# Folding a query weight with 32x32 matmul tiles and DMA turns, in a fused linear-attention and expert kernel

## The chip, the cores and the metric

The kernel runs on one core of one Trainium2 chip. The metric is the device time of one execution in microseconds (us). The kernel before was run three times: 270.49, 270.82 and 271.87 us, median 270.82 us.

## The reference, cut to what matters

```python
# x: [1, 2048, 1024], 32 heads of width 32
g = sigmoid((x * gate_w).sum(-1, keepdims=True))
q, k, v = split_heads(x @ wqkv)
pq, pk = q @ w_phi[h], k @ w_phi[h]                 # per head, 32 x 32
phi = lambda p: concat([softmax(p), softmax(-p)])   # 64 features a head
kv, z = phi(pk).T @ v, phi(pk).sum(0)
a = (phi(pq) @ kv) / (phi(pq) @ z + 1e-6) @ wo
# expert path: the one row of x with the largest router score
idx = argmax(x @ w_r); xs = x[idx]
y = (silu(xs @ w_gate) * (xs @ w_up)) @ w_down * sigmoid(r[idx])
b = x with y added to row idx
out = g * a + (1 - g) * b
```

Since `pq = x @ wq @ w_phi`, the kernel first multiplies the weights: the folded weight of a head is its 32 columns of `wq` times its 32x32 `w_phi`. The same is done for `wk`.

## The kernel before

The rows of x are 16 tiles of 128, and the depth 1024 is 8 blocks `kb` of 128. `xT` holds x transposed.

**V stage.** `v_first` computes V for tiles 0 and 1, and `k_v(t, c)` for the others, in three column groups c of 256, 384 and 386 columns (the last two columns of the 386 are the router score and the gate score, kept in `rg`). A tile is 24 matmuls. Between them lie the folds. `wT_load` brings one block of `wk` or `wq` transposed (a DMA transpose) into a quarter of one of the two `shv` buffers, six blocks at a time. `fold(which, wf, kb)` multiplies it: 8 matmuls of 128x128 whose moving operand is `BDm`, a block-diagonal matrix with four heads' `w_phi`, and two VectorE casts of 512 columns out of PSUM (tag `pB`) into `wkf` or `wqf`. `FOLDS[t]` says how many folds tile t has; all 16 lie in tiles 8 to 15, the key's first. At tile 15 `route()` finds the row with the largest router score: a TensorE transpose, VectorE max and index per tile, a small DMA (`mrow`) that brings the 16 candidates into one partition, VectorE again, then SyncE reads the index and loads that row (`rows`).

**K stage.** Steps i = 0 to 31 call `feats(i, wkf, False)`: 8 matmuls of 512 columns into a PSUM buffer (`pk`, pool `psA`, two buffers), two exponentials on ScalarE, sums and reciprocals on VectorE, the product phi on GpSimd or VectorE. From step 5 on `k_kv` accumulates phi times V into `kvps`, three PSUM banks that two memsets at the end of `v_first` prepared. At i = 7 `xs_turn` turns the loaded expert row on TensorE, and ScalarE spreads it into `xs32`; at i = 8, 14 and 21 `ffn_gu` multiplies it with the gate and up weights (32 or 48 matmuls of 512 columns with 32 weight columns each, four column positions of the array side by side). Their weights lie in buffers of 1 MB: `shv` (letter D), `ring` (A, three buffers) and a buffer for the later stores (W and V).

**Q stage.** Steps 32 to 63 do `feats` with `wqf` (`pq`), a DMA transpose of phi (`q_turn`), the numerator (`q_num`) and the output projection (`q_wo`), in an order that a table of times sets.

Each engine works through its own list in order; the lists are made ahead of the run. All DMAs that SyncE (SP) issues go into one hardware queue, q1.

Of the kernel before, what the change touches and what calls it, by code (L numbers as in the profile page):

```python
# [37 lines left out]
TX = 4  # L38
FOLDS = [0] * 8 + [1, 2, 2, 2, 2, 2, 2, 3]
TDV = 0  # L40


def general_path(tc, A_wqkv, A_w_phi, A_wo, x2, out2, gate, omg, y2, idx_pool, xT, wqf, ident, BDm):
# [46 lines left out]
    def features(w):  # L90
        for hf in range(2):
            for kb in range(KB):
                nc.tensor.matmul(pp[:].rearrange("p h f -> p (h f)"), lhsT=xTt[:, kb, :],
                                 rhs=w[:, kb, hf * 512:(hf + 1) * 512], start=(kb == 0), stop=(kb == KB - 1))
            nc.vector.tensor_reduce(out=mm[:, 0, :], in_=pp[:], axis=AX.X, op=ALU.max)
            nc.vector.tensor_reduce(out=mm[:, 1, :], in_=pp[:], axis=AX.X, op=ALU.min)
            for s in range(2):
                nc.vector.tensor_tensor(out=sh[:, s], in0=pp[:], in1=_bc(mm[:, s, :], [P, HH, DH]), op=ALU.subtract)
                nc.scalar.activation(out=sh[:, s], in_=sh[:, s], func=ACTF.Exp, scale=(1.0 if s == 0 else -1.0))
            nc.vector.tensor_reduce(out=sr[:], in_=sh[:], axis=AX.X, op=ALU.add)  # L100
            nc.vector.reciprocal(out=sr[:], in_=sr[:])
            for s in range(2):
                nc.vector.tensor_tensor(out=phi[:, hf * HH:(hf + 1) * HH, s, :], in0=sh[:, s],
                                        in1=_bc(sr[:, s, :], [P, HH, DH]), op=ALU.mult)

    with tc.For_i(0, S, P) as r0:
# [6 lines left out]
        features(wkf)  # L113
# [8 lines left out]
    with tc.For_i(0, NT, 1) as t:  # L122
# [3 lines left out]
        nc.vector.tensor_copy(out=gt[:, 1:2], in_=omg[:, bass.ds(t, 1)])  # L126
        features(wqf)
        for g in range(2):
# [36 lines left out]
def kernel(  # L165
# [130 lines left out]
    def wT_load(which, kb):  # L296
        n = (which * KB + kb) % 6
        wT[which, kb] = shv[n // 4][:, n % 4, :].rearrange("p (k f) -> p k f", f=P)
# [19 lines left out]
    def route():  # L318
# [152 lines left out]
    def ffn_gu(r, bufs):  # L471
        ws = [gu_load(r, k, b) for k, b in enumerate(bufs)]
        acc = psB.tile([P, 512], F32, name="facc", tag="pB")
# [79 lines left out]
    def v_first():  # L553
# [13 lines left out]
        for t in (1, 0):  # L567
            for c in range(3):
# [4 lines left out]
                v_out(t, c, acc[t, c])  # L573
        nc.vector.memset(kvps[:], 0.0)
        nc.vector.memset(kvps[:, 0:16 * KSTR].rearrange("p (r c) -> p r c", c=KSTR)[:, :, DH:66:DH + 1], 5e-7)

    kst = {}

    def feats(u, wf, is_q):
# [3 lines left out]
        for kb in range(KB):  # L583
            nc.tensor.matmul(pkf, lhsT=xT[:, kb, t * P:(t + 1) * P], rhs=wf[:, kb, hf * 512:(hf + 1) * 512],  # L584
                             start=(kb == 0), stop=(kb == KB - 1))
# [126 lines left out]
    def wload(n):  # L712
        wn["want"] += n
        while wq and wn["done"] < min(wn["want"], wn["folded"] + 6):
            wT_load(*wq.pop(0))
            wn["done"] += 1
# [16 lines left out]
    for t in range(TX, NT):  # L733
# [3 lines left out]
        for n, c in enumerate((2, 0, 1) if t == NT - 1 else (0, 1, 2)):  # L737
            k_v(t, c)
            if c == 2 and t == NT - 1:
                route()  # L740
            if n >= 3 - FOLDS[t]:
                w, kb = fq.pop(0)
                fold(w, wkf if w == 0 else wqf, kb)
                wn["folded"] += 1
                wload(1 if t + TX >= NT else 0)
    LAG = 5
# [142 lines left out]
```

## Time and profile before

| | |
|---|---|
| median of three runs | 270.82 us (270.49 to 271.87) |
| the profiled execution | 271.42 us |
| its span, first to last instruction | 269.7 us |
| TensorE (PE) busy | 262.7 us, 97% |
| VectorE (DVE) / ScalarE (ACT) / GpSimd (POOL) busy | 195.3 / 119.4 / 128.1 us |
| granted TensorE clock, mean | 0.996 of full speed |

The profile is of one execution, whose own time lies 0.6 us above the median of the runs. A matmul's recorded duration runs to the end of its pipeline, so that neighbours overlap; what a matmul costs TensorE is read from the distance between the starts of rows.

### The profile page before, as it was taken

Reading aid. Unit: us, or ns where it says so; the run is one execution under the profiler, and the core shown is the slowest. Engines: PE = TensorE matmul, PEld = TensorE weight load, DVE = VectorE, ACT = ScalarE, POOL = GpSimd, SP = SyncE. Lnnn points to the kernel's source line nnn. Section 1 sums busy time; section 2 is a strip of 40 time slices with the busy share of each in tenths; the row PEclk is TensorE's granted clock in tenths of the full one; section 3 lists DMA queues with packets and bytes.
Section 4 is the critical chain, followed back from the end, with each engine's and each line's share of the span. In section 5 each row is a group of like instructions: output and inputs, shape, how many; then the busy total and the mean of one; then the engine's idle time right before and its main releaser. Section 6 shows DMA issues by size and latency. Waiting matters only on the chain.

```text
span 269.7 us, 5422 instructions
## 1 busy us (share of the span) xinstructions
PE 262.7 (97%) x2023; PEld 143.6 (53%) x2023; DVE 195.3 (72%) x330; ACT 119.4 (44%) x243; POOL 128.1 (48%) x113
## 2 busy tenths in 40 slices
PE   8999999999999999999999999999999999999992
PEld 4666667777544555545554444455444454454441
DVE  3020015566789896999998999889889798888772
ACT  3154333333354554545546465545355544544110
POOL 6000000000096979739779997654555535554010
PEclk9999999999999999999999999999999999999998
DMA  6999999997950699669936899899997999899642
GB/s 237 240 149 187 182 190 322 157 191 195 416 205 0 202 414 394 243 202 381 355 85 228 166 176 209 180 209 198 224 207 156 181 212 168 204 138 232 138 120 62
DMA packets 102521, 56.35 MB, mean 209 GB/s; under 512 B 85132, under 2 KB 90332, under 8 KB 102492
## 3 DMA queue, kind: packets, MB, share of 16 engines
q1 hardware_dynamic: 99692, 51.29, 78.8%
q10 hardware_dynamic: 2768, 4.67, 6.4%
q8 instruction: 17, 0.28, 0.5%
q14 instruction: 12, 0.10, 0.1%
q0 software_dynamic: 32, 0.00, 0.0%
HBM read 31.27 MB, written 4.20 MB: 132 GB/s over the span
## 4 chain that ended last, share of the span: by engine, by line
PE 91%; DVE 5%; DMA 1%; ACT 1%; issue 1%; POOL 0%
PE po L693 20%; PE pk L584 20%; PE pv L542 18%; PE pq L584 17%; PE num L654 3%; PE kvps L620 3%; PE pW L307 3%; DVE ssum L592 3%; PE facc L478 2%; PE pv L564 1%; PE kvps L564 1%; DMA shv<-in_A_x_dram 1%; DVE rq L599 1%; DVE KV L629 1%; PE small_ps L496 1%
## 5 line engine op out<-in xcount | busy, mean ns | idle before, releaser
L592 DVE TENSOR_REDUCE ssum<-e 128x32 f32<-128x1024 bf16 x64 | 76.9, 1203 | 6.4 <-ACT e L588 6.2
L605 POOL TENSOR_TENSOR phi<-e,rq 128x1024 bf16<-128x1024 bf16 x32 | 61.0, 1913 | 40.4 <-DVE rq L599 32.9
L584 PEld LDWEIGHTS <-xT 128*128 128x128 bf16 x512 | 47.3, 97 | 52.6 <-issue 1.3
L584 PE MATMUL pq<-wqf,xT 128*128 128x512 bf16 x256 | 60.3, 379 | 0.0
L693 PE MATMUL po<-wo_sb,oT 128*128 128x512 bf16 (+2 forms) x264 | 60.0, 372 | 0.0
L584 PE MATMUL pk<-wkf,xT 128*128 128x512 bf16 x256 | 59.9, 379 | 0.0
L542 PE MATMUL pv<-wv_sb,xT 128*128 128x256 bf16 (+2 forms) x336 | 52.0, 307 | 0.0
L605 POOL TENSOR_TENSOR phi<-e,rs 128x1024 bf16<-128x1024 bf16 x25 | 47.8, 1912 | 2.3 <-DVE rs L599 1.4
L542 PEld LDWEIGHTS <-xT 128*128 128x128 bf16 x336 | 31.7, 97 | 14.1
L549 ACT CAST v_all<-pv 128x384 bf16<-128x384 f32 (+1 forms) x45 | 20.1, 448 | 40.8 <-PE pv L542 35.1
L587 ACT ACTIVATE e<-pq 128x512 bf16<-128x512 f32 x32 | 19.0, 594 | 42.7 <-PE pq L584 40.7
L693 PEld LDWEIGHTS <-oT 128*128 128x128 bf16 x264 | 23.8, 98 | 23.1
L587 ACT ACTIVATE e<-pk 128x512 bf16<-128x512 f32 x32 | 19.1, 597 | 29.2 <-PE pk L584 21.4
L309 DVE CAST wkf<-pW 128x512 bf16<-128x512 f32 x16 | 10.3, 686 | 28.1 <-PE pW L307 28.1
L420 POOL COPY wch<-shv 1x1 bf16<-1x1 bf16 x3 | 0.4, 178 | 57.4 <-DMA shv<-in_A_wqkv_dram 57.4
L697 DVE SCALAR_TENSOR_TENSOR oo<-po,gate,xg 128x512 bf16<-128x512 f32 (+2 forms) x33 | 24.0, 727 | 4.1 <-PE po L693 4.0
L602 POOL TENSOR_TENSOR ksum<-ksum,ssum 128x32 f32<-128x32 f32 x32 | 14.0, 438 | 22.0 <-DVE ssum L592 20.4
L659 DVE TENSOR_TENSOR o_sb<-num,rden 128x512 bf16<-128x512 f32 x32 | 21.7, 677 | 0.8
L588 ACT ACTIVATE e<-pk 128x512 bf16<-128x512 f32 x32 | 18.9, 591 | 0.0
L588 ACT ACTIVATE e<-pq 128x512 bf16<-128x512 f32 x32 | 18.9, 590 | 0.0
L678 ACT ACTIVATE xg<-xin,omg 128x1024 f32<-128x1024 bf16 x16 | 18.3, 1148 | 0.5
L654 PEld LDWEIGHTS <-phT 128*128 128x128 bf16 x256 | 12.3, 98 | 8.6 <-issue 1.1
(132 smaller groups left out, 201.3 us busy)
## 6 DMA issues: line engine op xcount, KB each, us to landing
wch<-in_B_w_down_dram SPq DMA_DIRECT2D x7, 1024.0 KB
wch<-in_B_w_up_dram SPq DMA_DIRECT2D x6, 1024.0 KB
wch<-in_B_w_gate_dram SPq DMA_DIRECT2D x4, 1024.0 KB
xin<-in_A_x_dram ACTq DMA_DIRECT2D x16, 256.0 KB
out_dram<-oo SPq DMA_DIRECT2D x30, 128.0 KB
wch<-in_B_w_gate_dram SPq DMA_DIRECT2D x4, 768.0 KB
wv_sb<-in_A_wqkv_dram SPq DMA_DIRECT2D x8, 256.0 KB
wo_sb<-in_A_wo_dram SPq DMA_DIRECT2D x1, 2048.0 KB
```

Source lines behind the costliest of these rows:

```text
L542: nc.tensor.matmul(pv[:, 0:hi - lo], lhsT=xT[:, kb, t * P:(t + 1) * P], rhs=wv_sb[:, kb, lo:hi], start=(kb == 0), stop=(kb == KB - 1))
L549: nc.scalar.copy(out=v_all[:, t, h0:h1, 0:DH], in_=pv[:, 0:(h1 - h0) * DH].rearrange("p (h d) -> p h d", d=DH))
L584: nc.tensor.matmul(pkf, lhsT=xT[:, kb, t * P:(t + 1) * P], rhs=wf[:, kb, hf * 512:(hf + 1) * 512], start=(kb == 0), stop=(kb == KB - 1))
L587: nc.scalar.activation(out=e[:, :, 0, :], in_=pk[:], func=ACTF.Exp)
L588: nc.scalar.activation(out=e[:, :, 1, :], in_=pk[:], func=ACTF.Exp, scale=-1.0)
L592: nc.vector.tensor_reduce(out=ssum[:], in_=e2, axis=AX.X, op=ALU.add)
L605: eng.tensor_tensor(out=phi[:].rearrange("p h s f -> p (h s) f"), in0=e2, in1=_bc(rs, [P, HH * 2, DH]), op=ALU.mult)
L654: nc.tensor.matmul(num[:, pl * 66:pl * 66 + 66], lhsT=phT[:, pl, :], rhs=KV[hf][:, pl, :], start=True, stop=True)
L659: nc.vector.tensor_tensor(out=st["o"][:, hf * HH:(hf + 1) * HH, :].rearrange("p (r h) d -> p r h d", h=2), in0=nv[:, :, :, 0:DH], in1=rden ...
L678: nc.scalar.activation(out=xg, in_=st["xin"][:], func=ACTF.Copy, scale=omg[:, t:t + 1])
L693: nc.tensor.matmul(po[:, 0:w], lhsT=st["oT"][:, kb, :], rhs=moe["wo"][:, kb, sl], start=(kb == 0), stop=(kb == KB - 1))
L697: nc.vector.scalar_tensor_tensor(out=o_out[:, 0:w], in0=po[:, 0:w], scalar=gate[:, t:t + 1], in1=st["xg"][:, sl], op0=ALU.mult, op1=ALU.add)
```

## The change

The fold of `wk` keeps its form, but lies in tiles 5 to 12, one to a tile, with eight `shv` quarters in place of six. The fold of `wq` is done the other way round by `qfold`: the weights are the 32x32 blocks `w_phi` and the moving operand is the loaded `wq` block, 512 columns (four kb of 128), so that the result is the folded weight transposed. Sixteen such matmuls, one for each of the 16 positions of 32 rows by 32 columns, make a pack; they write `kvps` (three banks) and one `pB` buffer. Four packs lie in tiles 13, 14 and 15 (`PACKS`). Two VectorE and two ScalarE copies take each pack to `wfT` (two `ring` buffers), and eight DMA transposes (`qfold_turn`, steps 1 to 8) turn it into `wqf`. Its column order is now by row position r first, so the moving operand of `pq` is read through `q_heads` in pieces of 32 columns.

The preparation of `kvps` moves to ScalarE (`kv_zero`, written at step 2). The second half of `route` becomes `route_row`, written at step 0 and held behind the first reciprocal of the K stage. The first expert loads (round 0) are written at step 0, and the buffers of all four rounds are dealt out anew.

```diff
-FOLDS = [0] * 8 + [1, 2, 2, 2, 2, 2, 2, 3]
+FOLDS = [0] * 5 + [1] * 8 + [0] * 3
+PACKS = {(13, 2): (0, 0), (14, 1): (1, 0), (15, 0): (0, 1), (15, 2): (1, 1)}
...
+def q_heads(wqf, kb, hf):
+    return wqf[:, kb, hf * 512:(hf + 1) * 512].rearrange("p (r c f) -> p c r f", r=4, f=DH)
...
-        n = (which * KB + kb) % 6
+        n = kb
...
+    def qfold(a, half):
+        if (a, half) == (0, 0):
+            moe["wfT"] = [ring.tile([P, 4, D], BF, name="wfT", tag="wch") for _ in range(2)]
+        pB = psB.tile([P, 512], F32, name="pW", tag="pB")
+        banks = [kvps[:, 0:512], kvps[:, 512:1024], kvps[:, 1024:1536], pB[:]]
+        for r in range(4):
+            for c in range(4):
+                j = 4 * a + c
+                nc.tensor.matmul(banks[r][32 * c:32 * c + 32, :].rearrange("p (k d) -> p k d", d=P),
+                                 lhsT=BDm[32 * r:32 * r + 32, j, 32 * r:32 * r + 32],
+                                 rhs=shv[half][32 * r:32 * r + 32, :, j * P:(j + 1) * P],
+                                 start=True, stop=True, tile_position=(32 * r, 32 * c), skip_group_check=True)
+        for r in range(4):
+            (nc.vector.tensor_copy, nc.scalar.copy)[r % 2](out=moe["wfT"][a][:, r, half * 512:(half + 1) * 512], in_=banks[r])
+
+    def qfold_turn(ar):
+        nc.sync.dma_start_transpose(out=wqf[:, :, ar * P:(ar + 1) * P], in_=moe["wfT"][ar // 4][:, ar % 4, :])
+
+    def kv_zero():
+        one = ones[:, 0:1]
+        nc.scalar.activation(out=kvps[:], in_=one.to_broadcast([P, 3 * 512]), func=ACTF.Copy, scale=0.0)
...
+    def route_row():
+        mrow = moe["mrow"]
         mxv = const.tile([1, 1], F32, name="mxv")
+        nc.vector.tensor_copy(out=mxv[:], in_=moe["rs"][0:1, 0:1])
...
-        nc.vector.memset(kvps[:], 0.0)
-        nc.vector.memset(kvps[:, 0:16 * KSTR].rearrange("p (r c) -> p r c", c=KSTR)[:, :, DH:66:DH + 1], 5e-7)
...
-            if c == 2 and t == NT - 1:
+            if n == 1 and t == NT - 1:
                 route()
...
-            ffn_gu(r, ("AAAD", "DWVA", "AADD")[r])
+            ffn_gu(r, ("WVDD", "AAAW", "VDDA")[r])
             if r == 2:
-                ffn_gu(3, "WV")
+                ffn_gu(3, "AA")
...
+        if i == 0:
+            moe["gu0"] = [gu_load(0, k, b) for k, b in enumerate("WVDD")]
         if i == 2:
+            kv_zero()
             gates()
+        if i == 0:
+            route_row()
+        if 1 <= i <= 8:
+            qfold_turn(i - 1)
```

Two places show how the lists of the engines change. ScalarE, from the gate's exponential at the end of the V stage into the K stage, before (the numbers behind the names keep the buffers apart):

```order
L313 ACTIVATE eg_1030<-rg_114 128x16
L549 CAST v_all_111<-pv_929 128x8x32
L549 CAST v_all_111<-pv_951 128x12x32
L587 ACTIVATE e_982<-pk_973 128x16x32
L588 ACTIVATE e_982<-pk_973 128x16x32
L587 ACTIVATE e_1001<-pk_992 128x16x32
L588 ACTIVATE e_1001<-pk_992 128x16x32
```

The same place of ScalarE's list in the changed kernel:

```order
L329 CAST wfT_779<-pW_865 128x512
L329 CAST wfT_779<-kvps_140 128x512
L583 CAST v_all_111<-pv_886 128x8x32
L583 CAST v_all_111<-pv_910 128x12x32
L329 CAST wfT_780<-pW_920 128x512
L329 CAST wfT_780<-kvps_140 128x512
L621 ACTIVATE e_950<-pk_941 128x16x32
L622 ACTIVATE e_950<-pk_941 128x16x32
L336 ACTIVATE kvps_140<-const-bfloat16-1.0 128x1536
L621 ACTIVATE e_1000<-pk_991 128x16x32
L622 ACTIVATE e_1000<-pk_991 128x16x32
L337 ACTIVATE kvps_140<-const-bfloat16-1.0 128x16x2
```

The copies of the last two packs stand ahead of the exponentials of step 0, and the long write of `kvps` between those of step 0 and step 1.

SyncE, from the last weight loads of the folds to the load of the expert row, before (`wch` is an expert weight buffer, `mrow` and `rows` the router's two DMAs):

```order
L299 DMA_TRANSPOSE shv<-in_A_wqkv_dram 128x8x128 x10
L454 DMA wch<-in_B_w_gate_dram 128x2x2048 x4
L333 DMA mrow<-mi 1x16x2
L454 DMA wch<-in_B_w_gate_dram 128x2x1536
L454 DMA wch<-in_B_w_up_dram 128x2x512
L344 TENSOR_LOAD ixi
L344 ISA x2
L345 ISA
L345 DMA rows<-in_A_x_dram 8x128
```

The same place of SyncE's list in the changed kernel:

```order
L304 DMA_TRANSPOSE shv<-in_A_wqkv_dram 128x8x128 x8
L488 DMA wch<-in_B_w_gate_dram 128x2x2048 x3
L488 DMA wch<-in_B_w_gate_dram 128x2x1536
L332 DMA_TRANSPOSE wqf<-wfT 128x8x128
L362 DMA mrow<-mi 1x16x2
L488 DMA wch<-in_B_w_gate_dram 128x2x2048
L332 DMA_TRANSPOSE wqf<-wfT 128x8x128 x4
L378 TENSOR_LOAD ixi
L378 ISA x2
L379 ISA
L379 DMA rows<-in_A_x_dram 8x128
L332 DMA_TRANSPOSE wqf<-wfT 128x8x128 x3
```

Five of the eight turns and a 1 MB expert load now stand between the last loads of the V stage and the load of the expert row.

## Rows read from the trace of the kernel before

**Rows 1.** The page's first part: busy us, share of the span, instructions.
```profile
PE 262.7 (97%) x2023; PEld 143.6 (53%) x2023; DVE 195.3 (72%) x330; ACT 119.4 (44%) x243; POOL 128.1 (48%) x113
```

**Rows 2.** The page's chain that ended last, shares by line.
```profile
PE po L693 20%; PE pk L584 20%; PE pv L542 18%; PE pq L584 17%; PE num L654 3%; PE kvps L620 3%; PE pW L307 3%; DVE ssum L592 3%; PE facc L478 2%; PE pv L564 1%; PE kvps L564 1%; DMA shv<-in_A_x_dram 1%; DVE rq L599 1%; DVE KV L629 1%; PE small_ps L496 1%
```

**Rows 3.** TensorE in order of time, end of the V stage: start, us, instruction.
```profile
66.06 0.61 PE L307 MATMUL pW<-BDm,shv 128*128 128x128 bf16 x8
66.51 0.82 PE L542 MATMUL pv<-wv_sb,xT 128*128 128x256 bf16 x6
67.32 0.23 PE L321 MATMUL small_ps<-ident,r_tm 128*128 128x128 bf16 x1
...
69.80 8.80 PE L584 MATMUL pk<-wkf,xT 128*128 128x512 bf16 x40
78.43 0.42 PE L620 MATMUL kvps<-v_all,phi 128*128 128x66 bf16 x8
```

**Rows 4.** TensorE in order of time around the first expert round.
```profile
84.37 0.17 PE L350 MATMUL small_ps<-ident,rows 128*128 128x8 bf16 x1
...
86.02 1.91 PE L478 MATMUL facc<-wch,xs 128*32 128x512 bf16 x32
87.87 0.82 PE L584 MATMUL pk<-wkf,xT 128*128 128x512 bf16 x3
```

**Rows 5.** TensorE in order of time, the two score columns of a first tile.
```profile
13.64 0.34 PE L571 MATMUL pv<-wv_sb,xT 128*128 128x2 bf16 x8
13.84 0.60 PE L542 MATMUL pv<-wv_sb,xT 128*128 128x256 bf16 x4
```

**Rows 6.** Groups by line and shape: count, busy us, mean ns, idle before and releaser.
```profile
L309 DVE CAST wqf<-pW 128x512 bf16<-128x512 f32 x16 | 10.5, 683 | 4.6 <-PE pW L307 4.5
L309 DVE CAST wkf<-pW 128x512 bf16<-128x512 f32 x16 | 10.3, 686 | 28.1 <-PE pW L307 28.1
...
L549 ACT CAST v_all<-pv 128x384 bf16<-128x384 f32 x30 | 14.5, 483 | 27.7 <-PE pv L542 27.7
...
L549 ACT CAST v_all<-pv 128x256 bf16<-128x256 f32 x15 | 5.6, 376 | 13.1 <-PE pv L542 7.4 <-PE pv L564 5.8
...
L478 PEld LDWEIGHTS <-xs 128*32 128x32 bf16 x112 | 2.7, 96 | 3.5 <-ACT xs L351 0.6 <-issue 0.4
...
L483 ACT COPY gs<-facc 128x512 f32<-128x512 f32 x4 | 2.3, 586 | 3.8 <-PE facc L478 3.8
```

**Rows 7.** ScalarE in order of time, first steps of the K stage.
```profile
71.72 0.60 ACT L587 ACTIVATE e<-pk 128x512 bf16<-128x512 f32 x1 [1.69 <-PE pk L584]
72.22 0.59 ACT L588 ACTIVATE e<-pk 128x512 bf16<-128x512 f32 x1
73.45 0.60 ACT L587 ACTIVATE e<-pk 128x512 bf16<-128x512 f32 x1 [0.64 <-PE pk L584]
```

**Rows 8.** SyncE's DMA issues in order of time: start, us of issue.
```profile
62.94 2.26 SPq L454 DMA_DIRECT2D wch<-in_B_w_gate_dram  x4
70.65 0.65 SPq L333 DMA_DIRECT2D mrow<-mi  x1
...
80.24 0.38 SPq L345 DMA_DIRECT2D rows<-in_A_x_dram  x1
```

**Rows 9.** Windows: busy us of PE, PEld, DVE, ACT, POOL; clock, DMA share, GB/s.
```profile
47.00:62.00 15.00, 15.00 (x141) 11.17 (x139) 9.02 (x14) 5.12 (x15) 0.00 (x0) 1.00 1.03 174
65.00:75.00 10.00, 10.00 (x74) 5.82 (x73) 8.04 (x22) 3.84 (x10) 0.66 (x2) 1.00 1.02 409
...
161.00:163.00 2.00, 2.00 (x29) 0.78 (x22) 2.00 (x6) 1.49 (x3) 1.79 (x2) 1.00 1.09 208
```

**Rows 10.** VectorE in order of time, the router's steps in the K stage.
```profile
76.57 0.16 DVE L335 TENSOR_REDUCE mxv<-mrow 1x1 f32<-1x16 f32 x1 [0.78 <-DMA mrow<-mi]
...
78.67 0.08 DVE L343 CAST ixi<-ixf 1x1 uint32<-1x1 f32 x1
```

**Rows 11.** GpSimd in order of time, the expert loads' gate copies.
```profile
62.74 0.41 POOL L420 COPY wch<-shv 1x1 bf16<-1x1 bf16 x3 [57.37 <-DMA shv<-in_A_wqkv_dram]
```

More of the change, by code (lines that the diff above doesn't have):

```diff
@@ L92, in features @@
             for kb in range(KB):
-                nc.tensor.matmul(pp[:].rearrange("p h f -> p (h f)"), lhsT=xTt[:, kb, :],
-                                 rhs=w[:, kb, hf * 512:(hf + 1) * 512], start=(kb == 0), stop=(kb == KB - 1))
+                nc.tensor.matmul(pp[:].rearrange("p (c r) f -> p c r f", r=4), lhsT=xTt[:, kb, :],
+                                 rhs=w(kb, hf), start=(kb == 0), stop=(kb == KB - 1))
             nc.vector.tensor_reduce(out=mm[:, 0, :], in_=pp[:], axis=AX.X, op=ALU.max)
@@ L112, in general_path @@
             nc.scalar.copy(out=va[:, hf * HH:(hf + 1) * HH, 0:DH], in_=pv[:])
-        features(wkf)
+        features(lambda kb, hf: wkf[:, kb, hf * 512:(hf + 1) * 512].rearrange("p (c r f) -> p c r f", r=4, f=DH))
         for pr in range(HH):
@@ L126, in general_path @@
         nc.vector.tensor_copy(out=gt[:, 1:2], in_=omg[:, bass.ds(t, 1)])
-        features(wqf)
+        features(lambda kb, hf: q_heads(wqf, kb, hf))
         for g in range(2):
@@ L309, in fold @@
             nc.vector.tensor_copy(out=wf[:, kb, jh * 512:(jh + 1) * 512].rearrange("p (j f) -> p j f", f=P), in_=pW[:])
+    def qfold(a, half):
[17 more added lines that the diff above has]
+        nc.scalar.activation(out=kvps[:], in_=one.to_broadcast([P, 3 * 512]), func=ACTF.Copy, scale=0.0)
+        nc.scalar.activation(out=kvps[:, 0:16 * KSTR].rearrange("p (r c) -> p r c", c=KSTR)[:, :, DH:66:DH + 1],
+                             in_=one.unsqueeze(2).to_broadcast([P, 16, 2]), func=ACTF.Copy, scale=5e-7)
     def gates():
@@ L333, in route @@
         nc.sync.dma_start(out=mrow[0:1, :, :], in_=mi[:])
+        moe["mrow"] = mrow
+    def route_row():
+        mrow = moe["mrow"]
         mxv = const.tile([1, 1], F32, name="mxv")
+        nc.vector.tensor_copy(out=mxv[:], in_=moe["rs"][0:1, 0:1])
         nc.vector.tensor_reduce(out=mxv[:], in_=mrow[:, :, 0], axis=AX.X, op=ALU.max)
@@ L471, in ffn_gu @@
     def ffn_gu(r, bufs):
-        ws = [gu_load(r, k, b) for k, b in enumerate(bufs)]
+        ws = moe.pop("gu0", None) or [gu_load(r, k, b) for k, b in enumerate(bufs)]
         acc = psB.tile([P, 512], F32, name="facc", tag="pB")
@@ L583, in feats @@
         for kb in range(KB):
-            nc.tensor.matmul(pkf, lhsT=xT[:, kb, t * P:(t + 1) * P], rhs=wf[:, kb, hf * 512:(hf + 1) * 512],
+            nc.tensor.matmul(pk[:].rearrange("p (c r) f -> p c r f", r=4) if is_q else pkf,
+                             lhsT=xT[:, kb, t * P:(t + 1) * P],
+                             rhs=q_heads(wf, kb, hf) if is_q else wf[:, kb, hf * 512:(hf + 1) * 512],
                              start=(kb == 0), stop=(kb == KB - 1))
@@ L713, in wload @@
         wn["want"] += n
-        while wq and wn["done"] < min(wn["want"], wn["folded"] + 6):
+        while wq and wn["done"] < min(wn["want"], wn["folded"] + 8):
             wT_load(*wq.pop(0))
@@ L744 @@
                 wn["folded"] += 1
-                wload(1 if t + TX >= NT else 0)
+                wload(4 if t + TX >= NT else 0)
+            if (t, n) in PACKS:
+                qfold(*PACKS[t, n])
     LAG = 5
```

## The prediction

> **What bounds the kernel now.** I read the page's busy times first: TensorE is busy for 262.7 of the span's 269.7 us [rows 1]. The reader should see that no other engine comes near, and then distrust the number, because neighbouring matmuls overlap in it. So the chain that ended last came second: the TensorE lines listed sum to 89% of it, spread over all stages, and the fold (`pW`, L307) is 3% of it [rows 2]. Third, TensorE in order of time: at the end of the V stage each row begins where the matmuls of the row before are issued, and nothing but one short gap lies between [rows 3]. The K stage begins at once, and its first 40 matmuls of 512 columns take 78.43 - 69.80 = 8.63 us, 0.216 each. Work taken from TensorE therefore comes off the end one for one, as long as nothing that it waits for becomes late; an engine with idle time gives nothing back.
>
> **What is taken away.** A fold block is eight 128x128 matmuls, 66.51 - 66.06 = 0.45 us on TensorE [rows 3]. The query's eight blocks are 8 x 0.45 = 3.6 us. The route's transpose stood 0.16 us late: six matmuls of 256 columns from 66.51 need 6 x 0.108 = 0.65 us and end at 67.16, and the transpose starts at 67.32 [rows 3]; it waited for `r_tm`, which stood on VectorE behind a fold cast. In the new place a third of a V tile lies between the score columns and the transpose, so I count this as saved. Together 3.74 us. The 16 VectorE casts to `wqf` (10.5 us) and the memsets go too, but VectorE sat idle for 28.1 us ahead of the fold casts [rows 6], so that is worth nothing by itself.
>
> **What the packs cost.** Four packs of 16 matmuls, each of 512 columns. No row of before has 32x32 tiles. The nearest is the expert round: 32 matmuls of 512 columns, four column positions side by side, take 87.87 - 86.02 = 1.85 us [rows 4], against 8 x 0.216 = 1.73 if the four ran wholly at once. So column positions do run together, with different moving data, and entering and leaving the form costs 0.12 us. For row positions the bounds are:
> - all 16 at once: one matmul and the entry, 0.216 + 0.12 = 0.34 us a pack, 1.3 us for four;
> - row positions one after another: 4 x 0.216 + 0.12 = 0.98 us a pack, 3.9 us for four.
>
> Between them lies issue. Eight pairs of weight load and two-column matmul take 13.84 - 13.64 = 0.20 us, 25 ns a pair [rows 5]. If the 16 matmuls start 25 ns apart, the last starts at 15 x 0.025 = 0.375, and the pack takes 0.375 + 0.216 + 0.12 = 0.71 us, 2.8 us for four. I take this one, since it rests on the only row that shows issue rather than columns.
>
> **Copies and PSUM.** A pack is emptied by two VectorE copies (0.69 us each, by the fold casts) and two on ScalarE (0.59 us, `gs`) [rows 6]. The next pack comes at least 2.2 us of V matmuls later, 1.4 us of copies, so TensorE should not wait for `kvps` or `pB`. The tightest is the last pack: one copy of the third stands on VectorE behind the router's `rT`, which waits for the transpose on TensorE, and is done about when the last pack begins; I cost it at nothing, at most 0.2.
>
> **`kv_zero` on ScalarE.** This is the new wait. Casts of 384 and 256 columns take 483 and 376 ns [rows 6], 0.84 ns a column, so 1536 columns take 0.483 + 1152 x 0.00084 = 1.45 us. It stands between the exponentials of steps 0 and 1. Let T be the start of step 0. Before, the first exponential begins at T + 1.92, the second 0.50 later, and step 1's at T + 3.65 [rows 3, 7]. Now `kv_zero` starts at about T + 2.92, step 1's exponentials at T + 4.27 and T + 4.77, and they end at T + 5.36. Step 3's matmuls need the PSUM buffer of step 1 (`psA` has two) at T + 3 x 1.73 = T + 5.18. TensorE waits 0.2 us and a hand-over: I take 0.3, bounds 0.1 and 0.5. Step 2's exponentials end by T + 6.6, ahead of step 4 at T + 7.2, so the delay does not go on. Behind them VectorE's sums and GpSimd's products shift too, but the first accumulation is at T + 8.63 [rows 3], and they are needed only there.
>
> **The queue.** The key's folds come earlier but are as many; their loads keep their places in q1, and the last query load is issued after the last key fold. A V tile is 8 x 1026 columns, 3.46 us at 0.216 per 512. With the new T of 68.9 (below) and three tiles and four packs between, that fold ends at about 68.9 - 10.4 - 2.8 = 55.7, some 9 us ahead of the third pack, which needs the load. What matters is the expert row. It is loaded at 80.24 and turned on TensorE at 84.37, T + 14.57 [rows 4, 8], with everything behind it in TensorE's list. In q1, `mrow` was issued at 70.65 and VectorE still waited for it at 76.57 [rows 8, 10]: 4 MB of expert loads issued from 62.94 lay ahead, and they move at 409 GB/s [rows 9], over 10 us. So small transfers wait their turn. New order: the gate copies, which waited for the last fold load until 62.74 [rows 11], can run once it lands, by my estimate at 59.2 (1.3 us of issue and some 2 us of landing after 55.8). Issued then, round 0 moves from about 61.3, with the 2 us that lay between 62.94 and the full window from 65 [rows 8, 9]; 2 MB + 1 MB + 0.75 MB at 409 GB/s end at about 71. Then turn 0, `mrow` (landing near 73.6, about when VectorE wants it), 1 MB until 75, and turns 1 to 4. A turn moves 0.26 MB. DMA transposes ran at 174 GB/s from DRAM and 208 GB/s from SBUF with the queue's engines full [rows 9]: 1.5 and 1.26 us each. The turns read SBUF, so I take 1.3: done at 80.2, and the row lands at about 81.7. With the new T = 69.80 - 3.74 + 2.8 = 68.9, the turn on TensorE is due at T + 14.57 + 0.3 = 83.7. Cover: 2.0 us. Cost nothing; with turns of 2 us it would be 1.5 us late. The turns themselves are due only at step 32, and rounds 1 to 3 find their buffers as early as before or earlier.
>
> **`pq` with pieces of 32 columns.** 256 matmuls at 0.216. No row shows a moving operand in pieces. I take no change; a loss of 5% would be 2.8 us.
>
> **The sum**, against the profiled execution's own 271.42 us: -3.74 + 2.8 + 0.3 = -0.6 us. On the median, 270.82, it gives 270.2 us. What can be told from no change is about 0.5%, 1.35 us.
>
> **The rivals.**
> - *All 16 positions at once.* For it: column positions do it [rows 4], row positions write different PSUM banks, and the weight loads can be issued ahead. Then -3.74 + 1.3 + 0.3 = -2.1: 268.7 us, faster. It decides below 0.48 us a pack, where the gain passes 1.35. Against it: 25 ns a pair [rows 5]. The Trainium skill, page "TensorE: Matmul & The Clock Gate", section on packing small matmuls, gives 10.6 times for 16 such tiles; an estimate from that, 16 x 0.216 / 10.6 = 0.33 us a pack, is this rival's time, and no run here shows it yet.
> - *Row positions one after another.* -3.74 + 3.9 + 0.3 = +0.5: 271.3 us, no change that can be told. For it: nothing in the trace shows row positions together.
> - *The expert row late.* If turns take 2 us, TensorE waits 1.5 us once: -0.6 + 1.5 = +0.9, 271.7 us. Against it: both transpose rates [rows 9].
> - *Weight loads in the open.* The other side. Every matmul of a pack goes to another tile with weights of its own. If each must first load them, at the 96 ns of a recorded 32-column load [rows 6], a pack takes 16 x 0.096 + 0.216 + 0.12 = 1.87 us, four 7.5, and the sum is -3.74 + 7.5 + 0.3 = +4.1: 274.9 us. It decides above 1.2 us a pack. Against it: in the expert round the same 96 ns loads are hidden at 58 ns a matmul [rows 4, 6]. The Trainium skill, page "TensorEngine Tiling (Array Packing)", says that column tiling excludes the fast weight load and that a change of tiling mode drains the engine; the 0.12 us of rows 4 agrees with a small drain, and no run here prices the weight load of 32x32 tiles.
>
> **How the numbers follow.** Chances: forecast 0.46, all at once 0.27, row positions serial 0.10, row late 0.07, weight loads in the open 0.08, pieces of 32 columns dear 0.02. The likeliest case by itself, with packs of 0.50 to 0.85 us and a ScalarE stall of 0.1 to 0.5, spans -1.6 to +0.2: 269.2 to 271.0 us. The range reaches down to the first rival, 268.5, and up past the second and third, 272.0; what is left out is the two dear cases and the tails. Faster by over 0.5%: the first rival and the lower edge of the forecast, 0.30. Slower: the two dear cases and the tail of a late row, 0.12. Within 0.5%: 0.58.
>
> **What would show it.** In the changed profile the packs are rows of 16 matmuls with 32 rows: the distance from the first to the next V or K matmul is the price, 0.34, 0.71, 0.98 or 1.87. A gap ahead of the matmuls of step 3, released by ScalarE's second exponential of step 1, shows the `kv_zero` term. The expert row's turn (`rows`) should begin right after the matmuls ahead of it; a gap there means that the queue was late. `pq` should stay at 0.216 us a matmul, as `pk` [rows 3]. The prediction fails if `pq` gets slower, if a pack waits for the copies of the one before, or if VectorE, busy for 8.0 of the 10 us around the stage's start [rows 9], meets the first steps later and hands the delay on.

## The result and the profile after

The changed kernel takes 273.73 us (median of 10 runs, 272.94 to 275.09); the kernel before took 271.88 us beside it (10 runs). The ratio over all runs is 1.0079 with a 95% interval of 1.0052 to 1.0105 (the two medians alone give 1.0068): slower by 0.8%. The prediction said 270.2, with a range that ended at 272.0. The profiled execution took 273.28 us, and its span is 271.3 us, 1.6 more than before.

The page of the changed kernel, busy times and the chain that ended last, which answer to [rows 1, 2]:

```profile
PE 261.9 (97%) x2023; PEld 140.5 (52%) x2023; DVE 190.4 (70%) x321; ACT 125.1 (46%) x253; POOL 128.3 (47%) x113
...
PE po L727 20%; PE pv L576 17%; PE pq L616 16%; PE pk L616 13%; DVE ssum L626 4%; PE num L688 3%; DMA gT<-gs 2%; PE facc L512 2%; PE kvps L654 2%; DMA mrow<-mi 2%; DMA oT<-o_sb 2%; PE pW L312 1%; PE pv L598 1%; PE kvps L598 1%; DMA shv<-in_A_x_dram 1%
```

TensorE is busy for 0.8 us less, and the chain names new members, three DMAs (`gT`, `mrow`, `oT`), and `pk` falls from 20% to 13%, since for a part of the K stage the chain no longer runs through TensorE. Where that happens, TensorE's rows in order of time show (start, us, instruction, idle before and releaser):

```profile
59.22 0.42 PE L324 MATMUL kvps<-shv,BDm 32*32 32x512 bf16 x12
...
59.58 2.35 PE L576 MATMUL pv<-wv_sb,xT 128*128 128x256 bf16 x16
61.89 0.43 PE L324 MATMUL kvps<-shv,BDm 32*32 32x512 bf16 x12
...
68.07 0.43 PE L324 MATMUL kvps<-shv,BDm 32*32 32x512 bf16 x12 [0.32 <-DVE wfT L329]
...
68.45 9.03 PE L616 MATMUL pk<-wkf,xT 128*128 128x512 bf16 x40
77.31 0.42 PE L654 MATMUL kvps<-v_all,phi 128*128 128x66 bf16 x8
...
79.58 0.43 PE L654 MATMUL kvps<-v_all,phi 128*128 128x66 bf16 x8
...
82.11 0.43 PE L654 MATMUL kvps<-v_all,phi 128*128 128x66 bf16 x8 [0.37 <-POOL phi L639]
...
85.33 0.18 PE L384 MATMUL small_ps<-ident,rows 128*128 128x8 bf16 x1 [1.06 <-DMA rows<-in_A_x_dram]
...
100.50 0.37 PE L473 MATMUL small_ps<-identf,gT 128*128 128x16 f32 x2 [1.15 <-DMA gT<-gs]
100.80 1.91 PE L512 MATMUL facc<-wch,xs 128*32 128x512 bf16 x32
```

The K stage starts at T = 68.45 and not 69.80 [rows 3]: the V stage is 1.35 us shorter, more than the prediction's 0.9. All of that and more is lost afterwards. Counted from T, since the start of the program differs a little between executions:

| us from T | before | after | after, without turns | reordered |
|---|---|---|---|---|
| first `kvps` row | 8.63 | 8.86 | 8.87 | 8.86 |
| third `kvps` row | 12.59 | 13.66 | 12.83 | 12.96 |
| turn of the expert row | 14.57 | 16.88 | 14.81 | 15.58 |
| second expert round (`facc`) | 28.85 | 32.35 | 29.40 | 29.71 |
| end of the span | 199.9 | 202.9 | 200.2 | 200.6 |

(The last two columns are experiments below; the second expert round of before starts at 98.65, its third `kvps` row at 82.39.) The loss has four places: 0.23 us ahead of the first accumulation, 0.84 ahead of the second and third, 1.24 more until the expert row's turn, and another 1.2 until the second round. Of the 3.5 us, some 0.5 come back by the end.

SyncE's issues of the changed kernel (start, us of issue):

```profile
66.71 2.37 SPq L332 DMA_TRANSPOSE wqf<-wfT  x1
69.17 0.65 SPq L362 DMA_DIRECT2D mrow<-mi  x1
69.92 0.52 SPq L488 DMA_DIRECT2D wch<-in_B_w_gate_dram  x1
70.50 11.17 SPq L332 DMA_TRANSPOSE wqf<-wfT  x4
83.78 0.38 SPq L379 DMA_DIRECT2D rows<-in_A_x_dram  x1
84.27 4.05 SPq L332 DMA_TRANSPOSE wqf<-wfT  x3
88.38 0.58 SPq L488 DMA_DIRECT2D wch<-in_B_w_up_dram  x1
...
91.88 2.59 SPq L521 DMA_DIRECT2D gT<-gs  x4
```

Turns 1 to 4 keep SyncE in issue for 11.17 us, 2.8 each on average where the prediction had 1.3. The read of the row's index stands behind them in SyncE's list: the row's load is issued at 83.78, at 80.24 before [rows 8]. Windows of the same stretch (busy us of PE, PEld, DVE, ACT, POOL; clock, DMA share, GB/s):

```profile
62.00:71.00 9.00, 8.68 (x93) 4.58 (x87) 5.62 (x17) 6.54 (x16) 0.18 (x1) 1.00 1.02 404
72.00:74.00 2.00, 1.94 (x10) 0.79 (x9) 1.22 (x3) 2.00 (x5) 1.00 (x2) 1.00 0.32 57
75.00:77.00 2.00, 2.00 (x11) 0.92 (x10) 1.59 (x4) 1.08 (x2) 0.16 (x1) 1.00 1.01 398
79.00:81.00 2.00, 1.87 (x17) 0.83 (x15) 1.93 (x3) 1.09 (x2) 1.59 (x3) 1.00 1.60 47
```

The last number of each row is to be read: the loads run at 404 GB/s, then for 2 us almost nothing moves (57), then the fourth 1 MB load (398), then again almost nothing (47), though turns are queued all the time. The number before it, the DMA engines' busy share, is 0.32 in the first of the two thin windows and 1.60 in the second, so that the two may not have one cause.

VectorE in the first steps of the K stage:

```profile
75.34 0.16 DVE L369 TENSOR_REDUCE mxv<-mrow 1x1 f32<-1x16 f32 x1 [2.06 <-DMA mrow<-mi]
...
75.88 1.20 DVE L626 TENSOR_REDUCE ssum<-e 128x32 f32<-128x1024 bf16 x1
```

The maximum over the candidates waits 2.06 us (0.78 before [rows 10]), and the sum of step 1 stands behind it in VectorE's list. So the small DMA holds up the main path: step 1's product on GpSimd runs at 77.61, T + 9.16 (T + 7.33 before), and TensorE's second and third accumulations wait for products. In the kernel before, the same sum had run ahead of that wait:

```profile
74.57 1.22 DVE L592 TENSOR_REDUCE ssum<-e 128x32 f32<-128x1024 bf16 x1
```

Counted from T, `mrow` comes hardly later than before: the maximum runs at T + 6.89, at T + 6.77 before. What is new is VectorE's list: `route_row` now stands ahead of that sum, so that an old wait costs time. It takes both: with the same list and no turns (e1_no_turns, below) the gaps ahead of the second and third accumulations are not there.

### The profile page after: what moved, and what is told of

The parts are those of the page before. It is cut to its first block, busy times and chain, and to the rows that moved or that the text cites. A ratio compares the mean times of both kernels' runs of the same rounds, so it can differ in the third digit from the quotient of the medians.

```text
span 271.3 us, 5441 instructions
## 1 busy us (share of the span) xinstructions
PE 261.9 (97%) x2023; PEld 140.5 (52%) x2023; DVE 190.4 (70%) x321; ACT 125.1 (46%) x253; POOL 128.3 (47%) x113
## 4 chain that ended last, share of the span: by engine, by line
PE 79%; DMA 8%; DVE 7%; SPq 1%; ACT 1%; issue 1%; POOL 0%; DVEq 0%; ACTq 0%
PE po L727 20%; PE pv L576 17%; PE pq L616 16%; PE pk L616 13%; DVE ssum L626 4%; PE num L688 3%; DMA gT<-gs 2%; PE facc L512 2%; PE kvps L654 2%; DMA mrow<-mi 2%; DMA oT<-o_sb 2%; PE pW L312 1%; PE pv L598 1%; PE kvps L598 1%; DMA shv<-in_A_x_dram 1%
## 5 line engine op out<-in xcount | busy, mean ns | idle before, releaser
L576 PE MATMUL pv<-wv_sb,xT 128*128 128x256 bf16 (+2 forms) x336 | 51.1, 307 | 0.0
```

The lines of the kernel that those rows point to most:

```text
L576: nc.tensor.matmul(pv[:, 0:hi - lo], lhsT=xT[:, kb, t * P:(t + 1) * P], rhs=wv_sb[:, kb, lo:hi], start=(kb == 0), stop=(kb == KB - 1))
```

## The experiments

Two theories stood at the start. Queue: the turns delay three small transfers (`mrow`, `rows`, `gT`), by SyncE's list and by the transfers ahead, and these delay TensorE. Copies: the new work on ScalarE and VectorE (copies of the packs, `kv_zero`) makes the first steps late. Nine kernels were run; each ratio is to the kernel before on the same chip, with its 95% interval.

| run | median us | ratio |
|---|---|---|
| the changed kernel | 273.73 | 1.0079 [1.0052, 1.0105] |
| e1_no_turns | 270.13 (10 runs) | 0.9976 [0.9960, 0.9992] |
| e2_loads_early | 277.68 (4 runs) | 1.0239 [1.0215, 1.0262] |
| e3_order | 270.22 (12 runs) | 0.9966 [0.9947, 0.9985] |
| e4_packs_twice | 275.68 (one run) | |
| e5_mrow_act | 276.78 (4 runs) | 1.0175 [1.0128, 1.0222] |
| e6_order_memset | 274.34 (6 runs) | 1.0120 [1.0084, 1.0156] |
| e7_order_again | 270.47 (12 runs) | 0.9979 [0.9958, 1.0000] |
| e8_row_by_act | 271.37 (10 runs) | 1.0014 [0.9992, 1.0036] |
| e9_late_turns | 288.76 (4 runs) | 1.0672 [1.0632, 1.0711] |

**e1_no_turns.** The eight turns are left out; the query's folded weights are filled with a constant, so the query features do not use them.

```diff
+    nc.gpsimd.memset(wqf[:], 0.01)
...
-        if 1 <= i <= 8:
-            qfold_turn(i - 1)
```

> The changed kernel without its eight DMA turns: wqf is filled with a constant by GpSimd early on, so the query features are not those of the weights. Theory A (the turns and the loads around them fill the one DMA queue, so that the small transfers mrow, rows and gT land late): the GpSimd waits at the second and third accumulation, the gap ahead of the turn of the expert row and the gap ahead of the second expert round go, 0.8 + 1.1 + 1.4 us, and the time falls from 273.3 to about 270.0 us. Theory B (the waits come from the copies and the PSUM write that moved onto ScalarE and VectorE): those stay, the gaps stay within 0.5 us, and the time falls by less than 0.7 us.

TensorE's row for the expert row, SyncE's issue of its load, and VectorE's wait:

```profile
83.26 0.17 PE L385 MATMUL small_ps<-ident,rows 128*128 128x8 bf16 x1
...
78.40 0.38 SPq L380 DMA_DIRECT2D rows<-in_A_x_dram  x1
...
74.09 0.16 DVE L370 TENSOR_REDUCE mxv<-mrow 1x1 f32<-1x16 f32 x1 [0.80 <-DMA mrow<-mi]
```

Up to the expert row's turn no gap is left but the first 0.23 us (table above), and 0.31 us more are lost before the second round (29.40 - 14.81 against 28.85 - 14.57). Packs, copies and `kv_zero` are all still in, so the copies are not the cause of the greater part. By the ratios the turns, with what they move in SyncE's list, cost 1.0% of the time, and without them the change is a gain of 0.24%.

**e2_loads_early.** The first two loads of round 0 no longer wait for the last fold load; all else stays.

```diff
-        gate_load(w[0:1, 0:1])
+        if where == "D":
+            gate_load(w[0:1, 0:1])
```

> Only the gate copies ahead of the first two expert loads (W and V) are taken away, so that these 2 MB move some 20 us earlier, in a stretch with idle DMA engines; the other loads and the turns then line up differently in the list: all eight turns and a further 1 MB load now stand ahead of the load of the expert row. Theory A1 (bytes in front are what counts): mrow lands 4 us sooner, VectorE no longer waits for it, the gap ahead of the expert row goes, 271 us or less. Theory A2 (the place in the queue counts): mrow lands sooner, but the expert row waits for eight turns and lands no sooner than before, so the gap ahead of its turn on TensorE stays 1 us or grows to 3; only the second round's wait (1.4 us) goes, since the turns end sooner: 272 to 273.5 us.

The waits for `mrow` and ahead of `kvps` went, as the queue theory has it. But the order of SyncE's list is made ahead by readiness, and it changed: all turns now stand ahead of the row's read (the row's turn waited 1.85 us), and the fourth buffer of round 0 was issued behind that, at 87.91. TensorE missed it in the middle of its first round:

```profile
98.33 1.03 PE L513 MATMUL facc<-wch,xs 128*32 128x512 bf16 x8 [3.55 <-DMA wch<-in_B_w_gate_dram]
```

Both forecasts (at most 271, and 272 to 273.5) were missed by over 4 us, since neither had the new list. It is the same data in another order: here what stands ahead of what sets the time, not the amount.

**e3_order and e7_order_again.** The order is set by other means: round 0's first two loads free, its two others into D and A, and round 1 opened by a D buffer held until the row's index is known.

```diff
-        gate_load(w[0:1, 0:1])
+        if r == 0 and where == "D":
+            gate_load(w[0:1, 0:1])
+        if r == 1 and where == "D":
+            nc.vector.tensor_copy(out=w[0:1, 0:1], in_=moe["ix"][0][:])
...
-            ffn_gu(r, ("WVDD", "AAAW", "VDDA")[r])
+            ffn_gu(r, ("WVDA", "DAAW", "VDDA")[r])
...
-            moe["gu0"] = [gu_load(0, k, b) for k, b in enumerate("WVDD")]
+            moe["gu0"] = [gu_load(0, k, b) for k, b in enumerate("WVDA")]
```

> The packs and turns as they are, with the queue put in another order: W and V loaded some 20 us earlier, round 0 in buffers W, V, D, A instead of W, V, D, D, round 1 in D, A, A, W, and the load into that D held until the router's index is known. Then one D and one A load (2 MB) stand ahead of the turns, and nothing but the turns between them and the expert row. Theory A: mrow lands by 72, the turns are through by 81, the row lands by 83, no gap ahead of its turn, no gap ahead of the second round; -3.3 us against the changed kernel, about 270.0, and 1 to 1.5 us below the kernel before. Theory B: within 0.7 us of the changed kernel.

> The reordered version once more, for a ratio to the kernel before from a second chip run and beside the version with the memset. If the gain of the first run (ratio 0.9966) is real, the ratio lies between 0.994 and 0.999 again: 269.6 to 270.7 us where the kernel before gives 271.2. If it was chance, the ratio lies within 0.2% of 1.

SyncE's issues, TensorE's row for the expert row, and a window over the turns, of e3_order:

```profile
70.05 10.08 SPq L332 DMA_TRANSPOSE wqf<-wfT  x7
...
82.13 0.38 SPq L379 DMA_DIRECT2D rows<-in_A_x_dram  x1
...
84.28 0.18 PE L384 MATMUL small_ps<-ident,rows 128*128 128x8 bf16 x1 [0.47 <-DMA rows<-in_A_x_dram]
...
72.00:77.00 5.00, 4.93 (x24) 2.17 (x23) 4.83 (x9) 4.13 (x8) 2.26 (x3) 1.00 1.01 187
```

Without a load between them seven turns take 10.08 us, 1.44 each, and move 187 GB/s. `mrow` lies ahead of them and VectorE waits for it no more; `gT` comes in time. The row is still 0.47 us late.

VectorE's next step on `mrow`, and GpSimd's product of step 0, show what the sum of step 1 waits for then:

```profile
73.76 1.68 DVE L371 TENSOR_SCALAR cnd<-mrow,mxv 1x16 f32<-1x16 f32 x1
```

```profile
73.50 1.91 POOL L642 TENSOR_TENSOR phi<-e,rs 128x1024 bf16<-128x1024 bf16 x1
```

The step on 16 numbers, 0.22 us in the changed kernel, now lasts until 75.44, when the product ends (75.41). So the sum starts at T + 6.86 with `mrow` in time, as in e1_no_turns and e8_row_by_act (T + 6.87 and T + 6.86), against T + 7.43 in the changed kernel: of VectorE's 2.06 us of waiting, an earlier `mrow` gives back 0.57.

By the ratios this version lies 1% below the changed kernel, and 0.34% and 0.21% below the kernel before in its two comparisons. The second interval ends at 1.0000, and the second ratio lies just outside the 0.2% that its expectation gave to chance, so the gain over the kernel before is small and likely, but not certain.

**e4_packs_twice.** Each pack's 16 matmuls are issued twice, to price a pack.

```diff
-        for r in range(4):
-            for c in range(4):
...
+        for _ in range(2):
+            for r in range(4):
+                for c in range(4):
...
```

> Every pack is computed twice in a row into the same PSUM banks (32 matmuls in place of 16); nothing else is changed. If all 16 positions run at once, the second half costs one matmul of 512 columns, about 0.22 us a pack. If the matmuls start 25 ns apart, it costs 0.40 us. If row positions run one after another, 0.86 us.

```profile
59.88 0.42 PE L325 MATMUL kvps<-shv,BDm 32*32 32x512 bf16 x12
...
60.11 0.41 PE L325 MATMUL kvps<-shv,BDm 32*32 32x512 bf16 x12
...
60.47 2.35 PE L577 MATMUL pv<-wv_sb,xT 128*128 128x256 bf16 x16
```

The second set of 16 begins 60.11 - 59.88 = 0.23 us after the first (0.21 to 0.23 in the four packs), the time of one matmul of 512 columns. That is the first of the three prices expected. The next V row begins 0.36 us after the second set, as it does after a single pack. The rest of this run's time does not speak of packs: its row was 2.64 us late.

**e5_mrow_act.** `mrow` goes out from ScalarE, into another hardware queue.

```diff
-        nc.sync.dma_start(out=mrow[0:1, :, :], in_=mi[:])
+        nc.scalar.dma_start(out=mrow[0:1, :, :], in_=mi[:])
```

> The changed kernel with the router's 16 candidates (mrow) issued by ScalarE, into another hardware queue; all else as in the changed kernel. Theory Q, small DMAs wait because of their place in SyncE's queue (behind 2 MB of expert loads and a turn): mrow arrives about 2 us after its issue, the maximum on VectorE waits at most 0.5 us instead of 2.06, the gaps of 0.29 and 0.55 us ahead of the second and third kvps rows go, the index is ready at about 75.5 instead of 77.5. The row's load still stands behind turns 1 to 4 in SyncE's list and is issued at 83 to 84 as before, and gT still behind 3 MB of loads, so the time falls by 0.6 to 0.8 us only, to 273.0. Theory M, the 16 DMA engines themselves are full and any queue waits as long: mrow takes 4 to 6 us on ScalarE's queue too, the wait stays above 1.2 us and the time is 273.7 or above.

```profile
70.57 0.62 ACTq L362 DMA_DIRECT2D mrow<-mi  x1
...
76.52 0.16 DVE L369 TENSOR_REDUCE mxv<-mrow 1x1 f32<-1x16 f32 x1 [1.41 <-DMA mrow<-mi]
...
75.58 10.00 SPq L332 DMA_TRANSPOSE wqf<-wfT  x4
```

The second theory of the expectation held: 76.52 - 70.57 = 5.95 us on the other queue, 75.34 - 69.17 = 6.17 on SyncE's. In this trace the place in one queue is not what `mrow` waits for. The time rose, since SyncE's list had changed again: two turns ahead of the 1 MB load, four behind it at 2.5 us each, and the row's turn waited 3.44 us. Behind that wait TensorE ran at half its clock, as the window of the first expert round shows (columns as above; the clock is the third number from the end):

```profile
91.40:94.70 3.30, 3.30 (x32) 1.08 (x32) 0.06 (x1) 0.00 (x0) 2.26 (x3) 0.53 0.94 284
```

From the row's turn to the accumulation behind that round it took 88.69 to 95.40, 6.71 us; the changed kernel, at a clock of 1.00, took 3.96. So the wait cost 2.75 us more behind it, nearly all at the low clock.

**e6_order_memset.** The reordered version with `kv_zero` on VectorE.

```diff
-        nc.scalar.activation(out=kvps[:], in_=one.to_broadcast([P, 3 * 512]), func=ACTF.Copy, scale=0.0)
+        nc.vector.memset(kvps[:], 0.0)
...
```

> The reordered version (first two loads ungated, W V D A, second round D A A W) with the preparation of kvps on VectorE (1.34 us memset) and not on ScalarE (1.46 us). Theory C, the 0.23 us that the first 40 matmuls of the K stage lose is ScalarE's write between the exponentials of steps 0 and 1: without it the distance from the first pk to the first kvps is 8.63 us, as in the kernel before, and the time falls by 0.2 us against the reordered version if VectorE can take it: 270.0. Rival D, VectorE pays: the memset stands ahead of the sums of step 0, the index comes 1.4 us later, the expert row's load with it, and its turn on TensorE waits 1 to 1.5 us longer: 271 or above.

ScalarE's first exponential of step 3, in the changed kernel and (second fence) with the memset on VectorE:

```profile
75.79 0.60 ACT L621 ACTIVATE e<-pk 128x512 bf16<-128x512 f32 x1 [0.87 <-PE pk L616]
```

```profile
75.54 0.60 ACT L622 ACTIVATE e<-pk 128x512 bf16<-128x512 f32 x1 [0.64 <-PE pk L617]
...
68.42 8.81 PE L617 MATMUL pk<-wkf,xT 128*128 128x512 bf16 x39
77.23 0.43 PE L655 MATMUL kvps<-v_all,phi 128*128 128x66 bf16 x8
...
86.86 0.18 PE L382 MATMUL small_ps<-ident,rows 128*128 128x8 bf16 x1 [3.50 <-DMA rows<-in_A_x_dram]
```

Step 3's exponential is at T + 7.34 with ScalarE's write and at T + 7.12 without it (76.90 - 69.80 = 7.10 before): the stall is ScalarE's, 0.2 us. But the first accumulation is hardly earlier (8.81): the sums stand behind the memset on VectorE, and GpSimd's product of step 0 begins at 75.26 (73.50 in e3_order) and takes 1.9. The index came at 80.50 where it had come at 77.07, and the row, with its load in SyncE's list behind two more expert loads, was 3.50 us late. The rival held, at more than twice its price. Part of that is the clock: it was 0.52 of full speed behind the wait (86.9 to 89.5), and from the row's turn to the accumulation behind the first expert round it took 5.57 us, 1.6 more than in the changed kernel.

**e8_row_by_act.** ScalarE reads the index and issues the row's load, at step 4.

```diff
-        idx_sp = nc.values_load(ixi[0:1, 0:1], engines=[ET.SP], min_val=0, max_val=S - 1)
-        nc.sync.dma_start(out=rows[0:KB, :], in_=x2[bass.ds(idx_sp, 1), :].rearrange("o (a b) -> (o a) b", b=P))
+    def row_load():
+        idx_sp = nc.values_load(moe["ix"][0][0:1, 0:1], engines=[ET.Activation], min_val=0, max_val=S - 1)
+        nc.scalar.dma_start(out=rows[0:KB, :], in_=x2[bass.ds(idx_sp, 1), :].rearrange("o (a b) -> (o a) b", b=P))
...
+        if i == 4:
+            row_load()
```

> The changed kernel, but the index of the expert row is read, and the row's load issued, by ScalarE behind the exponentials of step 3 in place of SyncE. Theory L, the row is late because SyncE's list has its read behind four turns that SyncE is still issuing: with the index ready at 77.4 the load is issued near 79.0 (1.6 us for the read, as before), the row is there when TensorE wants it, and the gap of 1.06 us ahead of its turn goes; ScalarE stands for some 2.5 us ahead of step 4, which costs TensorE 0.5 to 1 us once. The 2.06 us wait for mrow stays. Sum about 273.0, between 272.3 and 273.7. Theory Q, the transfer itself waits behind the turns' data on the DMA engines: issued near 79, it still lands at 84 to 85, and the gap of about 1 us stays on top of ScalarE's: 274.0 or above.

```profile
78.01 0.76 ACTq L382 DMA_DIRECT2D rows<-in_A_x_dram  x1
...
70.49 15.80 SPq L332 DMA_TRANSPOSE wqf<-wfT  x7
...
80.02 1.89 PE L618 MATMUL pk<-wkf,xT 128*128 128x512 bf16 x8 [0.20 <-ACT e L624]
...
83.73 0.17 PE L386 MATMUL small_ps<-ident,rows 128*128 128x8 bf16 x1
...
98.99 0.37 PE L475 MATMUL small_ps<-identf,gT 128*128 128x16 f32 x2 [1.04 <-DMA gT<-gs]
```

The index was ready at 76.93, the load issued 1.1 us later, and the row was there in time while SyncE was still in its turns. So its lateness was SyncE's list, not the DMA engines. ScalarE's stop cost TensorE some 0.35 us (the row released by it starts 0.61 behind the accumulation at 79.41, where 0.26 is usual). The time went from 0.8% slower to no difference that can be told; the 0.65% between the ratios are 1.8 us, and 271.37 lies below the expected 272.3 to 273.7. In the traces 1.24 us of it are the row's: from the third accumulation to the row's turn TensorE takes 1.98 us again, against 3.22. Most of the rest comes from `mrow`, which the edit does not touch: VectorE waited 1.44 us for it and not 2.06, and the second accumulation starts 1.99 us after the first, as before (1.98). So a wait of 1.44 us there costs TensorE nothing. `gT` was still 1.04 us late.

**e9_late_turns.** All turns are held until step 8, with buffers dealt out to suit.

```diff
-            ffn_gu(r, ("WVDD", "AAAW", "VDDA")[r])
+            ffn_gu(r, ("WVDD", "AWVD", "DAAA")[r])
...
-                ffn_gu(3, "AA")
+                ffn_gu(3, "WV")
...
+        if i == 8:
+            nc.gpsimd.tensor_copy(out=wqf[0:1, 0, 0:D:P], in_=xs32[0:1, 0:8, 0])
-        if 1 <= i <= 8:
-            qfold_turn(i - 1)
+        if 8 <= i <= 15:
+            qfold_turn(i - 8)
```

> The changed kernel with all eight turns held until the expert row has been spread (steps 8 to 15), and rounds 1 and 2 in buffers that are free by then (A W V D and D A A A, last two W V). Theory A, the whole loss of the first steps is turns ahead of small transfers: mrow waits 0.8 us as without turns, no gap ahead of the second and third kvps, the row's turn at T + 14.9 without a gap, gT ahead of the loads and on time. The turns then take about 11 us of the queue ahead of round 1's loads, whose first matmuls are due at T + 29.4, so TensorE waits there for wch, 1 to 3 us: 271 to 273 in all. Rival B, ScalarE's and VectorE's copies of the last packs make the first steps late: the kvps gaps of 0.29 and 0.55 us stay, and the time is 273.5 or above.

```profile
101.65 0.58 PE L473 MATMUL small_ps<-identf,gT 128*128 128x16 f32 x2 [3.76 <-DMA gT<-gs]
...
108.11 1.70 PE L512 MATMUL facc<-wch,xs 128*32 128x512 bf16 x8 [4.91 <-DMA wch<-in_B_w_gate_dram]
```

The first steps were free of gaps, as expected: third accumulation at T + 12.83, the row's turn at T + 14.82. But the releasing copy ran at 91.66, behind three products on GpSimd (what it reads was ready at 84.95), so that the turns began at 91.90, ahead of `gT` and of round 1's weights, and what was saved at T + 15 was paid several times at T + 33 and later. The expected 271 to 273 was missed by 16 us, because neither that list nor the round behind it had been costed.

## Why the prediction was wrong, point by point

**What is taken away, what the packs cost.** The V stage closes: -3.74, four packs at 0.36 to 0.38 us from their first matmul to the next V or K row (+1.5), the row ahead of each pack 0.11 to 0.15 us long (+0.5: the first V row between packs, 59.58 to 61.89, is 2.31 us for 8 x 640 columns, 2.16), and 0.32 of waiting give -1.4; measured -1.35. (3.6 and 0.16 are 3.76 and not 3.74, which changes nothing.) The term of 2.8 us was mis-sized, 2.0 measured, and its rival had the mechanism: all 16 positions at once. The rival's 1.3 was too low, since changing the form costs more than the 0.12 us a pack that both took from the expert round: 0.11 to 0.15 ahead of a pack and 0.13 to 0.17 behind it (0.36 to 0.38 less the 0.21 to 0.23 of a set). With both, a pack costs 0.5 us, just outside the 0.48 below which that rival was to decide. The row of 25 ns pairs [rows 5] was the wrong neighbour; the expert round [rows 4], which the prediction also had, was the right one. The Trainium skill's factor of 10.6 ("TensorE: Matmul & The Clock Gate", section on packing small matmuls), 0.33 us by the prediction's estimate, is near the 0.36 to 0.38 of a single pack; the second set of e4_packs_twice, 0.21 to 0.23, is better than that. Weight loads in the open would have given 1.87 and are excluded.

**Copies and PSUM.** Costed at nothing, at most 0.2 us; the last pack waited 0.32 for the VectorE copy of the third, at the place named.

**`kv_zero`.** 0.3 us forecast, 0.23 measured (8.86 - 8.63), and e6_order_memset shows that it is ScalarE's. ScalarE's write took 1.46 us (1.45 forecast). Mechanism and size were right.

**`pq` in pieces of 32 columns.** No change, as forecast: 379 ns a matmul, as `pk` has. The group of the changed kernel:

```profile
L616 PE MATMUL pq<-wqf,xT 128*128 128x512 bf16 x256 | 60.3, 379 | 0.0
```

**The queue. This step failed.** "A turn moves 0.26 MB ... I take 1.3: done at 80.2, and the row lands at about 81.7 ... Cover: 2.0 us. Cost nothing." With the measured packs, copies and `kv_zero`, and the queue at nothing, the sum is -3.74 + 2.0 + 0.32 + 0.23 = -1.2 us; e1_no_turns, which is just that kernel, came 1.05 us below the kernel before by the medians (270.13 against 271.18) and 0.65 by the ratio (0.2 to 1.1 by its interval). The rest, from a ratio of 0.9976 to 1.0079, 1.0% or 2.8 us, is this step. It went wrong in three ways:

- *The length of a turn.* 1.3 us came from the 208 GB/s of a 2 us window [rows 9], read as transposes alone. The DMA queues of that window (packets, MB, share of 16 engines):

```profile
q1 hardware_dynamic: 1019, 0.25, 73.1%
q10 hardware_dynamic: 80, 0.16, 35.7%
```

  The 0.16 MB of q10 are a load of `xin`; the transposes moved 0.25 MB, 125 GB/s on 73% of the engines' time. Where no load lies between the turns they took 1.35 to 1.48 (4.05/3 after, 10.08/7 e3_order, 8.87/6 e2_loads_early), so the rate was nearly right, in part by luck. In groups that begin behind a 1 MB load a turn took 1.9 to 2.8 us on average (7.61/4 e4_packs_twice, 15.80/7 e8_row_by_act, 10.00/4 e5_mrow_act, 11.17/4 after). And the prediction counted it as transfer time in a queue, while it was SyncE's own time: the read of the index behind it in the list could not begin. e8_row_by_act shows this: with the read on ScalarE, the row was in time while the turns went on. The rival "expert row late" had the place and, with turns of 2 us, a delay of 1.5; its chance of 0.07 was too small.
- *What stands behind `mrow`.* "Landing near 73.6, about when VectorE wants it": it came at 75.3, and the prediction did not look at VectorE's new list, in which step 1's sum stands behind the wait. That cost 0.29 + 0.55 us on TensorE. Its last sign of failing, VectorE handing a delay on, had the place but no price. It put the wait down to the place in q1; e5_mrow_act waited as long by another queue.
- *The third small transfer.* "Rounds 1 to 3 find their buffers as early as before or earlier": round 1's loads, 3 MB, were issued from 88.38 behind the last turns, and `gT` behind them at 91.88 (88.60 before). Two of the three `ring` buffers of that round hold `wfT` until the turns have read it, so loads into those two could not pass the turns. TensorE waited 1.15 us for `gT`. e8_row_by_act keeps that wait (1.04); e3_order, whose loads of that round go out from 80.66, has none.

## What to carry to other kernels

When DMAs are added to a queue that also carries small transfers on the main path, list for each small transfer what now stands ahead of it on the issuing engine, and cost the issuing engine's time, not only the bytes. Then look at what stands behind the instruction that waits for it, in the waiting engine's list. Moving a load or a wait lets a list made by readiness reorder itself, so that the new list must be read again after every such edit; e2_loads_early and e5_mrow_act lost more by that than the edit was worth.

## What the runs showed of the hardware

- Sixteen matmuls of 32x32 with weights of their own, in 16 positions, take the time of one: a second set starts 0.21 to 0.23 us after the first. Entering the form costs 0.11 to 0.15 us each time, and leaving it 0.13 to 0.17; the Trainium skill's drain at a change of tiling mode ("TensorEngine Tiling (Array Packing)", section "Key Properties") agrees with that.
- Where DMA turns and direct loads follow each other in one queue, the DMA engines of the changed kernel moved 57 and 47 GB/s in two windows of 2 us (72 to 74 and 79 to 81), against 187 for turns alone (e3_order) and some 400 for loads alone. Why is not settled; no run takes the queue apart at that place.
- From its issue until VectorE could use it, the 128-byte `mrow` took 5.95 us on ScalarE's queue and 6.17 behind loads and a turn in SyncE's. Behind loads alone it took 4.5 (e9_late_turns), 5.0 (e1_no_turns) and 5.9 (the kernel before), so that a turn ahead is not the whole of it.
- VectorE's small step `cnd` lasted until GpSimd's running product ended, within 0.03 us, in e1_no_turns, e2_loads_early, e3_order and e9_late_turns (0.91, 1.67, 1.68 and 1.40 us), against 0.12 before and 0.22 after, where no product ran beside it. The maximum just ahead of it kept its 0.16 us beside the product.
- Behind waits of TensorE of 3.44 us (e5_mrow_act), 3.50 (e6_order_memset), 3.55 (e2_loads_early) and 3.76 (e9_late_turns) the granted clock fell to 0.50 of full speed, the lower of its two levels (1.2 and 2.4 GHz), and rose again after 3.5 to 5 us of work in the first three; behind the 1.06 and 1.15 us of the changed kernel and the 2.64 of e4_packs_twice it stayed at 1.00. A long wait therefore cost more than its own length.
